# Value products of a softcapped attention in 64x64 quarters, two pairs of heads per turn

## The chip, the core and the metric

The program runs on one core of a Trainium2 chip. The metric is the device time of one execution in microseconds (us). The core's engines run side by side, each through its own list in program order, and wait for one another by semaphores: TensorE (PE, whose weight loads are shown as PEld), ScalarE (ACT), VectorE (DVE), GpSimd (POOL), and SyncE (SP), which here only issues DMAs.

## The reference

```python
# attention: 4 batches, 12 heads, 448 positions, 64 numbers per head
scores = q @ k.T / 8
scores = cap * tanh(scores / cap)
attn = exp(scores - max(scores)); attn = attn / (sum(attn) + 1e-9)
x = (attn @ v), heads side by side            # 1792 x 768
x = relu(x @ moe_w_in) ** 2 @ moe_w_out        # 768 -> 2048 -> 768
out = ((x @ w1) * (x @ w2)) @ w3 @ w_out       # 768 -> 1024 -> 1024 -> 768
```

## The kernel before

The program has two stages. The attention stage takes about the first 240 us; beside attention it multiplies w3 by the last w_out once, so that one product is left at the end ("weight products", L647 to L649: 384 columns, each a sum of three products of numbers split into a high and a low part). Then come the two dense blocks, in which PE works almost without a pause. The change is in the attention stage alone.

Two heads make a pair, two pairs make a quad: there are 24 pairs and 12 quads (d = 0 to 11). Scores are kept transposed, 128 keys on the partitions and 448 queries along each row. The 448 keys of a head are three tiles of 128 and a rest of 64. A *unit* is the two heads' tile of 128 keys (t = 0, 1, 2), or, once per quad, the four rests together (L, t = 3 in the code, `LAST`). So a quad has 7 units and the stage 84; before, their order in a quad is a0 a1 a2 L b0 b1 b2, where a and b are its pairs.

What happens to a unit u:

- `emit_qk`, L479 (L488 for L): four products in 64x64 quarters of PE's array, which run side by side, into a tile `sc` of two PSUM banks. There are two such tiles, so unit u+2 waits for the tanh of unit u.
- `emit_tanh` (L498) on ACT per unit, and `emit_exp` (L504) on ACT for two units at once.
- `emit_sum` (L514, L520) on DVE adds the tiles up over t for the denominators; `emit_den` (L559, and L563 for the first five quads) sums them over the partitions by a product with ones, once per quad.
- `emit_pv` (L533): the value products. For a tile of 128 keys two products of 128 rows by 64 columns of the array, one for each head; for L four of 64x64 (L540). All products of a pair add up in one PSUM bank `pv`, and `evacuate` (L569) copies the bank to `acc` on ACT or DVE.

The loop over u writes every engine's list in this order. At an even u: exp of the two units before, scores of u and u+1, their tanh, then some weight products. At an odd u: the copy of a finished weight product (L660), the value products of units u-5 and u-4, and what `later` holds for this u (copies of finished banks, denominators). I call one even and one odd u a *step*: step e has the scores of units 2e and 2e+1, and the value products of step e stand behind them in PE's list. Between these, pieces of the weights are converted on ACT, DVE and POOL (L119 to L144), and DVE multiplies `acc` by the inverse denominators (L353), which come by way of DRAM in DMAs (`dt`, `rec_d`, `bs`). q and k of a pair are loaded into one of two buffers (`load_qk`), v into one of three (`load_v`).

Of the kernel before, what the change touches and what calls it, by code (L numbers as in the profile page):

```python
# [9 lines left out]
F32 = mybir.dt.float32  # L10
# [4 lines left out]
AF = mybir.ActivationFunctionType  # L15
ALU = mybir.AluOpType
# [5 lines left out]
def tile_kernel(ctx, tc, q, k, v, cap, w_in, w_out, w1, w2, w3t, wo2, out):  # L22
# [31 lines left out]
    GD = 2  # L54
# [375 lines left out]
    with ExitStack() as actx:  # L430
# [13 lines left out]


        sel = stat.tile([128, 32 + GD - 1], F32, name="sel")

        def what(u):

            d, x = divmod(u, 7)  # L450
            return 2 * d + (x > LAST), x if x <= LAST else x - LAST - 1

        def load_qk(p, first=S):

            if p < NPAIR:
                b, hp = divmod(p, NP)
                rk = ap_.tile([128, S], F32, name="rk", bufs=2)
                rq = ap_.tile([128, S], F32, name="rq", bufs=2)
                SP.dma_start(out=rk[:, :first], in_=k[b, hp, :, :first])
                SP.dma_start(out=rq, in_=q[b, hp])  # L460
                if first < S:
                    SP.dma_start(out=rk[:, first:], in_=k[b, hp, :, first:])
                loaded[p] = rk, rq

        def load_v(p):
            if p < NPAIR:
                b, hp = divmod(p, NP)
                vals[p] = ap_.tile([128, NT, D], F32, name="rv", bufs=3)
                SP.dma_start(out=vals[p], in_=v[b, hp])

        def emit_qk(u):

            p, t = what(u)
            sc = ps_s.tile([128, 2, 512], F32, name="sc")
            if t < LAST:
                rk, rq = loaded[p]
                for z, j in product(range(2), range(2)):
                    r, c = slice(j * D, (j + 1) * D), j ^ z
                    PE.matmul(sc[c * D:(c + 1) * D, j, :S], rk[r, 128 * t + c * D:128 * t + (c + 1) * D], rq[r, :], start=True,  # L479
                              stop=True, tile_position=(j * D, c * D))  # L480
                if p % 2 and t == LAST - 1:
                    load_qk(p + 2)
            else:
                for z in range(2):
                    rk, rq = loaded[p + z]
# [4 lines left out]
                load_qk(p + 2)  # L490
# [14 lines left out]

        def emit_sum(u):

            p, t = what(u)
            if t == 0:
                return  # L510
            if t == 1:
                sums[p] = ap_.tile([128, 2, S], F32, name="sum", bufs=3)
            if t < LAST:
                DVE.tensor_tensor(out=sums[p], in0=units[u - 1] if t == 1 else sums[p], in1=units[u], op=ALU.add)  # L514
            z = p % 2
            if p // 2 >= LAST_ADDED and (t == LAST or z and t == 1):
                x = units[u - z * 2]
                for j in range(2):
                    r = slice((j ^ z) * D, (1 + (j ^ z)) * D)
                    DVE.tensor_tensor(out=sums[p][r, j, :], in0=sums[p][r, j, :], in1=x[r, z, :], op=ALU.add)  # L520

        def pv_tile(p):
            pvs[p] = ps_v.tile([128, 512], F32, name="pv")[:, :S]

        def emit_pv(u):

            p, t = what(u)
            x = units[u]
            if t < LAST:
                if t == 0 and p % 2 == 0:  # L530
                    pv_tile(p)
                for j in range(2):
                    PE.matmul(pvs[p][j * D:(j + 1) * D], vals[p][:, 3 * j + t, :], x[:, j, :],  # L533
                              start=t == 0 and p % 2 == 0, stop=t == LAST - 1 and p % 2 == 1, tile_position=(0, j * D))
            else:
                pv_tile(p + 1)
                for z in range(2):
                    for j in range(2):
                        r = slice((j ^ z) * D, (1 + (j ^ z)) * D)
                        PE.matmul(pvs[p + z][j * D:(j + 1) * D], vals[p + z][r, 6, :], x[r, z, :],  # L540
                                  start=z == 1, stop=z == 0, tile_position=((j ^ z) * D, j * D))

        def den_group(p):

# [4 lines left out]
        def emit_den(p):  # L549

            b, g, n = den_group(p)
            c = p % NP // 2 - g
            if c == 0:
                dens[b] = ps_d.tile([128, 512], F32, name="den")[:, :S]
            for z in range(2):
                ps = sums.pop(p + z)
                for j in range(2):
                    r = 32 * (2 * z + j)
                    PE.matmul(dens[b][r:r + 32], sel[:, GD - 1 - c:GD - 1 - c + 32], ps[:, j, :],  # L559
                              start=c == 0, stop=c == n - 1 and p // 2 >= LAST_ADDED, tile_position=(0, r))  # L560
            for z, j in product(range(2), range(2)) if p // 2 < LAST_ADDED else ():
                r, h = 32 * (2 * z + j), slice((j ^ z) * D, (1 + (j ^ z)) * D)
                PE.matmul(dens[b][r:r + 32], sel[h, GD - 1 - c:GD - 1 - c + 32], units[7 * (p // 2) + LAST][h, z, :],  # L563
                          start=False, stop=c == n - 1, tile_position=(h.start, r))

        def evacuate(p):
# [119 lines left out]
        for n in range(3):  # L686
            w_fetch(n)
        load_v(0)
        wprod = w_products()
        wnext, chains, side = 0, [], []  # L690
        products_left = NM * 16
# [2 lines left out]

        later = {}
        for d in range(NPAIR // 2):
            for x, p in ((7 * d + LAST, 2 * d), (7 * d + 6, 2 * d + 1)):
                later.setdefault((x + 4 | 1) + EVAC, []).append(partial(evacuate, p))
            x = (7 * d + 12 | 1) + 2 * (d == NPAIR // 2 - 1)
            later.setdefault(x, []).append(partial(emit_den, 2 * d))  # L700
            later.setdefault(x + EVAC, []).append(partial(store_den, 2 * d))

        for u in range(NU + 10):
            if u < NU and u % 7 in (1, 4):
                load_v(what(u)[0] + 1)
            if 0 <= u - 1 < NU:
                emit_exp(u - 1)
            if u % 2 == 0:
                if u < NU:
                    for x in (u, u + 1):  # L710
                        emit_qk(x)
                    for x in (u, u + 1):
                        emit_tanh(x)
                if w_open:
# [477 lines left out]
```

## Time and profile before

| | |
|---|---|
| median of 3 runs | 1018.32 us (1018.26 to 1018.82) |
| the profiled execution | 1018.64 us, of which the span from its first to its last instruction is 1016.8 |
| PE busy | 1002.5 us, 99% of the span |
| DVE, ACT, POOL busy | 790.1, 549.4, 207.5 us |
| granted PE clock | full (1.00) |

An execution of 1018.64 us is 1.8 us longer than its span. In rows of a timeline a matmul in 32-bit numbers counts as two, so that the four quarter products of a unit appear as x8, and the two 128x64 products as x4; the order of the program counts them once. The end of a matmul is modelled, since matmuls overlap; intervals between starts are what can be relied on. "[1.45 <-PE sc L479]" behind a row says how long its engine had been idle and what ended that.

### The profile page before, as it was taken

The numbers are of one execution on the slowest core, as the hardware profiler recorded it, in microseconds if no ns is written. First come the engines' busy times: TensorE is split into PE (matmuls) and PEld (weight loads), VectorE is DVE, ScalarE is ACT, GpSimd is POOL, SyncE is SP. The second block draws the span as 40 slices with busy tenths as digits, with TensorE's granted clock in tenths as the row PEclk, the third lists the DMA queues.
The fourth block names the chain that finished last, engine by engine and source line by source line (L and its number), as shares of the span: only waits on it lengthen the run. The fifth ranks groups of instructions, "written<-read, shape, count | busy, mean of one in ns | idle before, by whom it ended". The sixth has DMA issues, their size and how long they took to land.

```text
span 1016.8 us, 15085 instructions
## 1 busy us (share of the span) xinstructions
PE 1002.5 (99%) x5410; PEld 827.3 (81%) x5410; DVE 790.1 (78%) x1494; ACT 549.4 (54%) x952; POOL 207.5 (20%) x367
## 2 busy tenths in 40 slices
PE   7999999999999999999999999999999999999998
PEld 1343455566999999999999999999999999999997
DVE  5967988786677989888888887558557788947796
ACT  7999978776786566556655665343241122241100
POOL 3332222221211111111111101002232230333220
PEclk9999999999999999999999999999999999999999
DMA  6567566645456756567576554206577673987662
GB/s 217 180 203 218 179 205 208 198 139 204 125 151 194 223 174 199 188 186 233 171 205 211 175 164 147 63 1 189 166 218 228 208 231 104 332 252 229 215 206 109
DMA packets 82591, 189.35 MB, mean 186 GB/s; under 512 B 10738, under 2 KB 34676, under 8 KB 82516
## 3 DMA queue, kind: packets, MB, share of 16 engines
q0 software_dynamic: 42896, 104.25, 33.1%
q1 hardware_dynamic: 39476, 84.14, 27.1%
q8 instruction: 43, 0.70, 0.3%
q14 instruction: 32, 0.26, 0.1%
q10 hardware_dynamic: 144, 0.00, 0.0%
HBM read 144.53 MB, written 43.82 MB: 185 GB/s over the span
## 4 chain that ended last, share of the span: by engine, by line
PE 86%; DVE 6%; ACT 5%; DMA 1%; issue 1%; POOL 0%; SPq 0%; DVEq 0%; POOLq 0%; ACTq 0%
PE h L361 13%; PE h L360 13%; PE h L362 13%; PE y L361 10%; PE y L360 10%; PE y L362 9%; PE sc L479 3%; PE pv L533 3%; PE h L647 2%; PE h L649 2%; PE h L648 2%; ACT pt L498 1%; ACT pt L504 1%; DVE sum L514 1%; PE y L1007 1%
## 5 line engine op out<-in xcount | busy, mean ns | idle before, releaser
L361 PE MATMUL y<-gl,wb 128*128 128x448 f32 x372 | 135.0, 363 | 0.0
L360 PE MATMUL y<-gh,wb 128*128 128x448 f32 x372 | 134.9, 363 | 0.0
L362 PE MATMUL y<-gh,wb 128*128 128x448 f32 x372 | 134.0, 360 | 0.0
L412 DVE TENSOR_TENSOR acc<-y,acc 128x448 f32<-128x448 f32 x168 | 97.9, 619 | 18.3 <-PE y L362 17.1
L230 POOL DMA_DIRECT2D wc_d<-bs x56 | 30.6, 546 | 268.2 <-DVE bs L86 125.9
L86 DVE TENSOR_TENSOR gl<-gr,gh 128x448 fp32r<-128x448 f32 x78 | 48.4, 620 | 46.7 <-ACT gh L395 42.7
L393 ACT ACTIVATE gr<-h 128x448 f32<-128x448 f32 x62 | 33.4, 539 | 90.0 <-PE h L362 89.6
L360 PEld LDWEIGHTS y<-gh,wb 128*128 128x128 f32 x372 | 69.8, 188 | 5.8 <-ACT acc L410 0.4
L479 PE MATMUL sc<-rq,rk 64*64 64x448 f32 x576 | 66.2, 566 | 8.2 <-DMA rq<-q 4.8
L122 ACT ACTIVATE cvx<-raw 128x384 int32<-128x384 uint32 (+1 forms) x136 | 73.8, 543 | 0.0
L843 POOL DMA_DIRECT2D wb<-wc_d x112 | 59.6, 545 | 68.7 <-PE h L362 43.6
L362 PEld LDWEIGHTS y<-gh,wb 128*128 128x128 f32 x372 | 69.6, 187 | 4.8
L361 PEld LDWEIGHTS y<-gl,wb 128*128 128x128 f32 x372 | 69.8, 188 | 3.7
L361 PE MATMUL h<-x1l,wb 128*128 128x448 f32 x192 | 69.7, 363 | 0.0
L361 PE MATMUL h<-x2l,wb 128*128 128x448 f32 x192 | 69.7, 363 | 0.0
L360 PE MATMUL h<-x1h,wb 128*128 128x448 f32 x192 | 69.5, 362 | 0.0
L360 PE MATMUL h<-x2h,wb 128*128 128x448 f32 x192 | 69.4, 362 | 0.0
L362 PE MATMUL h<-x1h,wb 128*128 128x448 f32 x192 | 69.3, 361 | 0.0
L362 PE MATMUL h<-x2h,wb 128*128 128x448 f32 x192 | 69.3, 361 | 0.0
L119 ACT ACTIVATE cvx<-raw 128x384 f32<-128x384 f32 x124 | 66.8, 539 | 0.0
L360 PE MATMUL h<-x0h,wb 128*128 128x448 f32 x180 | 65.2, 362 | 0.3 <-DVE bt L924 0.3
L142 ACT ACTIVATE wb<-cvx 128x384 fp32r<-128x384 f32 x56 | 29.1, 519 | 67.3 <-DVE cvx L130 39.8
(232 smaller groups left out, 2589.6 us busy)
## 6 DMA issues: line engine op xcount, KB each, us to landing
wb<-wc_d POOLq DMA_DIRECT2D x112, 384.0 KB, 5.7
wc_d<-bs POOLq DMA_DIRECT2D x56, 384.0 KB, 3.2
raw<-wy_d POOLq DMA_DIRECT2D x48, 384.0 KB, 3.6
raw<-w_in SPq DMA_DIRECT2D x32, 384.0 KB, 3.6
raw<-w_out SPq DMA_DIRECT2D x32, 384.0 KB, 3.6
raw<-w SPq DMA_DIRECT2D x32, 384.0 KB, 3.9
wy_d<-spare POOLq DMA_DIRECT2D x25, 384.0 KB, 4.4
raw<-w3t SPq DMA_DIRECT2D x16, 384.0 KB, 4.1
```

The costliest lines, as they stand in the source:

```text
L86: DVE.tensor_tensor(out=l, in0=src, in1=h.bitcast(F32), op=ALU.subtract)
L119: ACT.activation(a, upper, AF.Copy, scale=2.0 ** -112)
L122: ACT.activation(r, words[:, :, 0], AF.Copy, scale=2.0 ** -29)
L230: POOL.dma_start(out=wc_d[m, j], in_=x)
L360: PE.matmul(ps, wh, xh[:, i, :], start=start and i == 0, stop=False)
L361: PE.matmul(ps, wh, xl[:, i, :], start=False, stop=False)
L362: PE.matmul(ps, wl, xh[:, i, :], start=False, stop=(i == n - 1))
L393: ACT.activation(r, h, AF.Relu)
L412: DVE.tensor_tensor(out=a, in0=y, in1=a, op=ALU.add)
L479: PE.matmul(sc[c * D:(c + 1) * D, j, :S], rk[r, 128 * t + c * D:128 * t + (c + 1) * D], rq[r, :], start=True, stop=True, tile_position=(j ...
L533: PE.matmul(pvs[p][j * D:(j + 1) * D], vals[p][:, 3 * j + t, :], x[:, j, :], start=t == 0 and p % 2 == 0, stop=t == LAST - 1 and p % 2 == ...
L843: POOL.dma_start(out=x, in_=wc_d[s % NM, j])
```

## The change

- **Order of the units.** In a quad with even d: a0 a1 b0 b1 L a2 b2; with odd d: a0 b0 a1 b1 L a2 b2. `order` and `unit_of` hold it; sums and denominators look units up there.
- **Value products.** `emit_pv` goes, `emit_turn` comes. In step e the table `GROUPS` (14 steps, repeated three times; an entry is step, quad, half, tiles) says which quad has its turn, which half, and which t. A turn goes over t and for each t issues four 64x64 products (L574, in `pv_product`): both heads of both pairs, each with 64 of the 128 keys. These four use the four quarters of the array. The other 64 keys of the tiles come in another turn, with the other `half`. L is taken whole as before. I call four quarter products one *round*; a quad has 7 rounds, as many as before (where two 128x64 products were one). The last quad is done as before, in 128x64 products, behind all units (L563 of the new file).
- **A wait.** If the quad has already had a turn, the first product of the turn waits for the tanh of unit 2e ("fence" below).
- **PSUM banks** of both pairs are taken together, and both are copied out right behind the quad's last turn; before, each pair's copy came one step after its last product.
- **Loads.** Three tiles from the pool `cv` are a third buffer for q and k (every third pair) and a fourth for v (every fourth). `load_qk(p + 3)` is issued with the last scores of pair p; v of a quad is loaded when the quad two before it is done.

```diff
+        third = [cv.tile([128, S], F32, name="bt", bufs=3) for _ in range(3)]
+        ORDERS = "a0 a1 b0 b1 L a2 b2", "a0 b0 a1 b1 L a2 b2"
...
+        GROUPS = [(3, 0, 0, "01"), (4, 0, 1, "01"), (5, 0, 0, "2L"), (6, 0, 1, "2"), (7, 1, 0, "01L"), (8, 1, 1, "012"), (9, 1, 0, "2"),
...
-                if p % 2 and t == LAST - 1:
-                    load_qk(p + 2)
+                if t == LAST - 1:
+                    load_qk(p + 3)
...
-            ACT.activation(pt, units[u], AF.Tanh, scale=scl)
+            tanhs[u] = ACT.activation(pt, units[u], AF.Tanh, scale=scl)
...
+        def emit_turn(e):
...
+            d, half, what = turns[e]
+            if "0" in what and 2 * d not in pvs:
+                pv_tile(2 * d)
+                pv_tile(2 * d + 1)
...
+            fence = tanhs[2 * e]
+            for t, z, j in product(what, range(2), range(2)):
+                t = LAST if t == "L" else int(t)
+                i = pv_product(2 * d + z, j, j ^ z ^ (0 if t == LAST else half), t, d not in begun and t == 0, done_at[d] == e and t == (LAST if what[-1] == "L" else int(what[-1])))
+                if fence and d in begun:
+                    tc.add_manual_dep(i.ins, fence.ins.name, mybir.DependencyInfo(mybir.DependencyClass.Sync, mybir.DependencyReason.DATA),
+                                      reason="the other row half of the array has finished with this bank")
+                fence = None
+            begun.add(d)
...
+        def pv_product(p, j, h, t, start, stop):
...
+            r = slice(h * D, (h + 1) * D)
...
+            v, x = (vals[p][r, 6, :], units[unit_of[d, LAST]][r, p % 2, :]) if t == LAST else (vals[p][r, 3 * j + t, :], units[unit_of[p, t]][r, j, :])
+            return PE.matmul(pvs[p][j * D:(j + 1) * D], v, x, start=start, stop=stop, tile_position=(r.start, j * D))
...
-            for x, p in ((7 * d + LAST, 2 * d), (7 * d + 6, 2 * d + 1)):
-                later.setdefault((x + 4 | 1) + EVAC, []).append(partial(evacuate, p))
+            for z in range(2):
+                later.setdefault(2 * done_at[d] + 1, []).append(partial(evacuate, 2 * d + z))
+                later.setdefault(2 * done_at[d] + 3, []).append(partial(load_v, 2 * d + 4 + z))
...
-                for x in (u - 5, u - 4):
-                    if 0 <= x < NU:
-                        emit_pv(x)
+                emit_turn(u // 2)
```

Three places show what moves. The first is PE's list from the value products of step 15 to the denominators of step 16. Before (`pv` rows are value products, `sc` rows scores, `h` rows weight products, `den` denominators):

```order
L533 MATMUL pv<-pt,rv 64x448 x4
L479 MATMUL sc<-rq,rk 64x448 x8
L647 MATMUL h<-wb,w3h 128x384
L648 MATMUL h<-wb,w3h 128x384
L649 MATMUL h<-wb,w3l 128x384
L533 MATMUL pv<-pt,rv 64x448 x4
L559 MATMUL den<-sum,sel 32x448 x4
L563 MATMUL den<-pt,sel 32x448 x4
```

And after, from the last of the four rounds of step 15 on (`bt` are the new buffers):

```order
L574 MATMUL pv<-pt,rv 64x448 x2
L574 MATMUL pv<-pt,bt 64x448 x2
L503 MATMUL sc<-bt 64x448 x2
L503 MATMUL sc<-rq,rk 64x448 x2
L494 MATMUL sc<-bt 64x448 x4
L680 MATMUL h<-wb,w3h 128x384
L681 MATMUL h<-wb,w3h 128x384
L682 MATMUL h<-wb,w3l 128x384
L574 MATMUL pv<-pt,rv 64x448 x2
L574 MATMUL pv<-pt,bt 64x448 x2
L592 MATMUL den<-sum,sel 32x448 x4
L596 MATMUL den<-pt,sel 32x448 x4
```

Step 15 had two rounds and has four, step 16 had two and has one, and between value products and scores the shape of the products no longer changes.

The second place is PE's list around step 30, which has no weight products. Before, from the value products of step 29 to the scores of step 31:

```order
L533 MATMUL pv<-pt,rv 64x448 x4
L479 MATMUL sc<-rq,rk 64x448 x8
L533 MATMUL pv<-spare,rv 64x448 x4
L559 MATMUL den<-sum,sel 32x448 x4
L479 MATMUL sc<-rq,rk 64x448 x8
```

And after, from the third of step 29's four rounds:

```order
L574 MATMUL pv<-pt,rv 64x448 x2
L574 MATMUL pv<-pt,bt 64x448 x2
L574 MATMUL pv<-pt,rv 64x448 x2
L574 MATMUL pv<-pt,bt 64x448 x2
L503 MATMUL sc<-rq,rk 64x448 x2
L503 MATMUL sc<-bt 64x448 x2
L494 MATMUL sc<-rq,rk 64x448 x4
L574 MATMUL pv<-pt,rv 64x448 x2
L574 MATMUL pv<-pt,bt 64x448 x2
L592 MATMUL den<-sum,sel 32x448 x4
L494 MATMUL sc<-bt 64x448 x4
L494 MATMUL sc<-rq,rk 64x448 x4
```

The value products of step 30, which now wait for the tanh of unit 60, stand directly behind the scores of units 60 and 61.

The third place is ACT's list at the end of the stage, where the operands of the first dense block are split (`x0h`, `x1h`; `gh` is its first result). Before:

```order
L569 ACTIVATE acc_72<-pv 128x448
L504 ACTIVATE spare<-spare,capt 128x1792
L322 ACTIVATE x0h<-acc_69 128x448 x3
L569 ACTIVATE acc_72<-pv 128x448
L322 ACTIVATE x0h<-acc_69 128x448 x3
L322 ACTIVATE x1h<-acc_70 128x448 x2
L393 ACTIVATE cvx<-sc 128x448
L394 ACTIVATE cvx<-cvx 128x448
L395 ACTIVATE gh_2510<-cvx 128x448
L569 ACTIVATE acc_72<-pv 128x448
L322 ACTIVATE x1h<-acc_70 128x448 x4
```

And after:

```order
L602 ACTIVATE acc_72<-pv 128x448
L518 ACTIVATE spare<-spare,capt 128x1792
L322 ACTIVATE x0h<-acc_69 128x448 x3
L602 ACTIVATE acc_72<-pv 128x448 x2
L322 ACTIVATE x0h<-acc_69 128x448 x3
L322 ACTIVATE x1h<-acc_70 128x448 x2
L393 ACTIVATE cvx<-sc 128x448
L394 ACTIVATE cvx<-cvx 128x448
L395 ACTIVATE gh_2622<-cvx 128x448
L322 ACTIVATE x1h<-acc_70 128x448 x4
```

The last pair's copy has moved from behind `gh` to before the second three of `x0h`.

## Rows read from the trace of the kernel before

**Rows 1.** Stretches: start:end length, busy us of PE, PEld, DVE, ACT, POOL; clock.

```profile
10.00:50.00 40.00, 36.77 (x267) 10.94 (x263) 35.77 (x65) 38.17 (x42) 14.96 (x11) 1.00 0.61 194
50.00:100.00 50.00, 49.45 (x348) 18.74 (x340) 36.98 (x72) 49.07 (x63) 12.85 (x24) 1.00 0.69 203
...
150.00:200.00 50.00, 50.00 (x338) 28.65 (x336) 38.42 (x75) 39.82 (x55) 12.72 (x24) 1.00 0.61 190
```

**Rows 2.** What PE waited for up to 250 us: total, times, longest.

```profile
PE sc L479 <- DMA rq<-q: 4.8, 1, 4.8
```

**Rows 3.** Groups by form: quarter value products, busy us, mean ns.

```profile
L540 PE MATMUL pv<-pt,rv 64*64 64x448 f32 x64 | 7.9, 562 | 0.0
```

**Rows 4.** Timeline of PE, step 31 to 32: start, length, instructions.

```profile
166.29 0.97 PE L533 MATMUL pv<-spare,rv 128*64 128x448 f32 x4
167.19 0.98 PE L540 MATMUL pv<-spare,rv 64*64 64x448 f32 x8
167.99 1.68 PE L479 MATMUL sc<-rq,rk 64*64 64x448 f32 x16
169.60 0.44 PE L647 MATMUL h<-wb,w3h 128*128 128x384 f32 x1
```

**Rows 5.** Timeline of PE, steps 13 to 16.

```profile
63.06 1.72 PE L533 MATMUL pv<-spare,rv 128*64 128x448 f32 x8
...
66.49 1.73 PE L479 MATMUL sc<-rq,rk 64*64 64x448 f32 x16
...
76.24 1.72 PE L533 MATMUL pv<-pt,rv 128*64 128x448 f32 x8
77.89 1.74 PE L479 MATMUL sc<-rq,rk 64*64 64x448 f32 x16
```

**Rows 6.** Timeline of ACT: tanh of steps 10, 13, 16 and 17.

```profile
49.97 1.91 ACT L498 ACTIVATE spare<-sc,scl 128x896 f32<-128x896 f32 x2 [1.45 <-PE sc L479]
...
63.84 1.91 ACT L498 ACTIVATE pt<-sc,scl 128x896 f32<-128x896 f32 x2
...
78.94 1.91 ACT L498 ACTIVATE spare<-sc,scl 128x896 f32<-128x896 f32 x2
...
84.75 1.91 ACT L498 ACTIVATE spare<-sc,scl 128x896 f32<-128x896 f32 x2 [0.92 <-PE sc L479]
```

**Rows 7.** Chain of waits, 80 to 125 us: start, length, what.

```profile
81.03 0.53 DVE acc L569
...
87.90 4.74 DMA rec_d<-dt
...
93.72 6.40 DMA bs<-rec_d
...
118.34 0.44 DVE cvt L130
118.80 0.42 ACT w3h L142
...
124.53 0.39 ACT cvt L660
```

**Rows 8.** Timeline around step 30, PE and ACT.

```profile
157.00 1.72 PE L533 MATMUL pv<-pt,rv 128*64 128x448 f32 x8
...
160.10 1.89 ACT L498 ACTIVATE pt<-sc,scl 128x896 f32<-128x896 f32 x2
```

**Rows 9.** Timeline of PE behind the attention stage.

```profile
243.21 0.47 PE L361 MATMUL sc<-x0l,wb 128*128 128x448 f32 x1 [0.59 <-DVE x0l L86]
...
251.25 0.48 PE L361 MATMUL sc<-gl,wb 128*128 128x448 f32 x1 [0.66 <-DVE gl L86]
```

**Rows 10.** Timeline of DVE: copies behind quads 0 and 1, a pause.

```profile
32.54 0.61 DVE L569 COPY acc<-pv 128x448 f32<-128x448 f32 x1
...
45.36 0.62 DVE L569 COPY acc<-pv 128x448 f32<-128x448 f32 x1
...
66.09 0.42 DVE L86 TENSOR_TENSOR w3l<-cvt,w3h 128x256 fp32r<-128x256 f32 x1 [3.54 <-ACT w3h L142]
```

More of the change, by code (lines that the diff above doesn't have):

```diff
@@ L446, in tile_kernel @@
         sel = stat.tile([128, 32 + GD - 1], F32, name="sel")
-        def what(u):
-            d, x = divmod(u, 7)
-            return 2 * d + (x > LAST), x if x <= LAST else x - LAST - 1
+        tanhs, begun = {}, set()
+        third = [cv.tile([128, S], F32, name="bt", bufs=3) for _ in range(3)]
+        ORDERS = "a0 a1 b0 b1 L a2 b2", "a0 b0 a1 b1 L a2 b2"
+        order = []
+        for d in range(NPAIR // 2):
+            for x in ORDERS[d % 2].split():
+                order.append((2 * d, LAST) if x == "L" else (2 * d + (x[0] == "b"), int(x[1])))
+        unit_of = {x: u for u, x in enumerate(order)}
+        GROUPS = [(3, 0, 0, "01"), (4, 0, 1, "01"), (5, 0, 0, "2L"), (6, 0, 1, "2"), (7, 1, 0, "01L"), (8, 1, 1, "012"), (9, 1, 0, "2"),
+                  (10, 2, 1, "01"), (11, 2, 0, "01L"), (12, 2, 1, "2"), (13, 2, 0, "2"), (14, 3, 1, "01"), (15, 3, 0, "01L2"), (16, 3, 1, "2")]
+        turns, done_at = {}, {}
+        for c, (e, d, half, what) in product(range(NPAIR // 8), GROUPS):
+            e, d = e + 14 * c, d + 4 * c
+            if 2 * e < NU:
+                turns[e] = d, half, what
+            done_at[d] = e
+        turns[NU // 2], turns[NU // 2 + 1] = (NPAIR // 2 - 1, None, "01"), (NPAIR // 2 - 1, None, "L2")
+        done_at[NPAIR // 2 - 1] = NU // 2 + 1
         def load_qk(p, first=S):
@@ L456, in load_qk @@
                 b, hp = divmod(p, NP)
-                rk = ap_.tile([128, S], F32, name="rk", bufs=2)
-                rq = ap_.tile([128, S], F32, name="rq", bufs=2)
+                rk, rq = third[:2] if p % 3 == 2 else (ap_.tile([128, S], F32, name=x, bufs=2) for x in ("rk", "rq"))
                 SP.dma_start(out=rk[:, :first], in_=k[b, hp, :, :first])
@@ L467, in load_v @@
                 b, hp = divmod(p, NP)
-                vals[p] = ap_.tile([128, NT, D], F32, name="rv", bufs=3)
+                vals[p] = third[2].rearrange("p (t d) -> p t d", t=NT) if p % 4 == 3 else ap_.tile([128, NT, D], F32, name="rv", bufs=3)
                 SP.dma_start(out=vals[p], in_=v[b, hp])
         def emit_qk(u):
-            p, t = what(u)
+            p, t = order[u]
             sc = ps_s.tile([128, 2, 512], F32, name="sc")
@@ L506, in emit_sum @@
         def emit_sum(u):
-            p, t = what(u)
+            p, t = order[u]
             if t == 0:
@@ L513, in emit_sum @@
             if t < LAST:
[L514 to L518, printed above, removed]
+                DVE.tensor_tensor(out=sums[p], in0=units[unit_of[p, 0]] if t == 1 else sums[p], in1=units[u], op=ALU.add)
+            if p // 2 < LAST_ADDED:
+                return
+            w = unit_of[p - p % 2, LAST]
@@ L519, in emit_sum @@
+            for z in range(2) if t == LAST else (p % 2,) if t == 1 and w < u else ():
+                for j in range(2) if p - p % 2 + z in sums else ():
                     r = slice((j ^ z) * D, (1 + (j ^ z)) * D)
-                    DVE.tensor_tensor(out=sums[p][r, j, :], in0=sums[p][r, j, :], in1=x[r, z, :], op=ALU.add)
+                    x = sums[p - p % 2 + z][r, j, :]
+                    DVE.tensor_tensor(out=x, in0=x, in1=units[w][r, z, :], op=ALU.add)
         def pv_tile(p):
             pvs[p] = ps_v.tile([128, 512], F32, name="pv")[:, :S]
[L525 to L541, printed above, removed]
@@ new lines, in emit_turn @@
+        def emit_turn(e):
+            if e not in turns:
+                return
+            d, half, what = turns[e]
+            if "0" in what and 2 * d not in pvs:
+                pv_tile(2 * d)
+                pv_tile(2 * d + 1)
+            if half is None:
+                for t in what:
+                    if t == "L":
+                        for z, j in product(range(2), range(2)):
+                            pv_product(2 * d + z, j, j ^ z, 3, False, False)
+                        continue
+                    for p, j in product((2 * d, 2 * d + 1), range(2)):
+                        PE.matmul(pvs[p][j * D:(j + 1) * D], vals[p][:, 3 * j + int(t), :], units[unit_of[p, int(t)]][:, j, :],
+                                  start=t == "0", stop=t == "2", tile_position=(0, j * D))
+                return
+            fence = tanhs[2 * e]
[7 more added lines that the diff above has]
+            begun.add(d)
@@ L703, in tile_kernel @@
         for u in range(NU + 10):
-            if u < NU and u % 7 in (1, 4):
-                load_v(what(u)[0] + 1)
+            if u in (1, 5, 7):
+                load_v({1: 1, 5: 2, 7: 3}[u])
             if 0 <= u - 1 < NU:
@@ L709, in tile_kernel @@
                 if u < NU:
-                    for x in (u, u + 1):
-                        emit_qk(x)
+                    emit_qk(u)
+                if u < NU:
+                    emit_qk(u + 1)
                     for x in (u, u + 1):
```

5 lines of the change are left out of this document (3 added, 2 removed).

## The prediction

> **What bounds the kernel now.** I read the view of stretches first. After 50 us PE is busy for 49.45 and 50.00 of 50 us, in the dense blocks too, so what the change is worth is the time by which the attention stage, about 240 us, ends earlier or later. The first 100 us are a close race of three: ACT is busy for 49.07 of the 50 us up to 100, and DVE for 35.77 of the 40 up to 50 [rows 1]. Then PE alone is full. Next the list of what PE waited for: in 250 us one DMA, at the very start [rows 2]. A third buffer for q and k has no wait to remove, and I cost it at nothing: by the code they are issued three units or more ahead of their use, after as before. Third the timelines, PE beside ACT. In the first 105 us ACT has hardly a gap but two where it waits for scores, 1.45 and 0.92 us, both after a step with denominators [rows 6]; there PE is the late one. Last the chain of waits from 80 to 125 us: it runs through a copy of value products on DVE at 81.03, two DMAs of the inverse denominators, a stretch of DVE and then ACT, which ends with the copy of a weight product at 124.53 [rows 7]. PE's next weight products start at 124.96, since they need that bank. So up to 125 us a saving on PE alone is not one of time; from 125 us to the end PE is the bound.
>
> **Work of the array: unchanged.** A round is four 64x64 products after and two 128x64 products before, seven to a quad in both. From 166.29 to 167.19 a round and a change of shape take 0.90 us; from 167.19 to 169.60 a round of 64x64 value products, two rounds of 64x64 scores and a change take 2.41 [rows 4]. So a round is (2.41 - 0.90) / 2 = 0.755 us and a change of shape 0.145; two rounds of 128x64 and a change, 76.24 to 77.89, are 1.65 [rows 5], a change of 0.14. I take 0.15. Twice as many weight loads cost nothing, since PEld has 28.65 busy us in 50 [rows 1].
>
> **Changes of shape.** Value products and scores now have the same shape. Counted in PE's list, up to the first product of the dense block, 136 changes become 96. Of the 40 that go, 25 stand ahead of the weight products of step 25 (124.96 us), where the chain holds the end, and 15 behind: 15 x 0.15 = -2.25 us. If quarter products of different kinds drained like different shapes, it would be 0 (rival C).
>
> **Rounds that come later.** Value products start one step later (step 3 for step 2) and the table shares them out unevenly. Up to step 24 the old list has 23 steps x 2 = 46 rounds, the new one 44 (28 in the first fourteen steps, then 2, 2, 2, 1, 3, 3, 1, 2). Two rounds move from where PE is not the bound to where it is: 2 x 0.755 = +1.5 us.
>
> **The fence.** The first product of a turn now waits for the tanh of unit 2e, except in a quad's first turn. What is queued behind it on PE is the rest of the turn, denominators and the next scores, for which ACT waits. From step 25 on the steps with weight products have 6 to 24 of them ahead of it, and the tanh is over in time. Two fenced steps have none (30 and 36). In step 30: turn 29 starts at 157.00 [rows 8] and now has four rounds, so the scores of unit 60 start at 157.00 + 4 x 0.755 = 160.0 and PE is through with both units at 161.5. A tanh starts 1.05 after its scores (77.89 to 78.94 [rows 5, 6]) and lasts 1.0 (two take 1.91): it ends at 162.05, a wait of 0.55. ACT, which reached it at 160.10 before [rows 8], doesn't make it later. Step 36 has three rounds ahead and comes to about the same: together +1.1. Bounds: 0, if the tanh comes sooner behind its scores, and 2 x 1.0, a whole tanh each.
>
> **The stage in which ACT and DVE share the bound.** Here I follow steps 13 to 16. In step 13 the value products started at 63.06, before that step's tanh at 63.84 [rows 5, 6]. Now they wait for its first half, until 64.85, and one round and the denominators (66.49 - 63.06 - 1.65 = 1.8) bring the next scores to 67.4 instead of 66.49. From there to 76.24 PE had no pause; two changes fewer leave turn 15 at 76.85. It has four rounds where two were: the scores of step 16 start at 79.85 instead of 77.89, their tanh at 80.9 instead of 78.94, and turn 16, fenced on it, starts at 81.9 and ends at 82.7. Behind it DVE's copy of the bank, which ran at 81.03 in the midst of DVE's own work, now waits till then: +1.7 us at a link of the chain to 124.53, and a link has no slack in it [rows 7]. So the weight products of step 25 start 1.7 later. In return step 16 has one round before its denominators instead of two, and ACT's later waits go.
> The bounds: the best is that both waits of ACT go, since every step with denominators now has one round, and the fence costs nothing: -(1.45 + 0.92) = -2.4. The worst adds DVE's copies behind quads 0 and 1: they ran at 32.54 and 45.36 [rows 10], in a stretch where DVE has few gaps, and would wait for fenced turns too, for as long as the third at most: 2 x 1.7, so +5.1. I take +1.7: DVE stood idle for 3.54 us before 66.09 [rows 10], where the first two can be made up, but not the third.
>
> **The end of the stage.** Eight rounds with denominators follow the last weight products where six did; the two more are counted above. PE's waits there, 0.59 and 0.66 us [rows 9], are for operands that ACT and DVE split; PE arrives later against them, so the first goes. The last pair's copy no longer stands on ACT behind `gh`, ahead of the work that the second wait hangs on: of that I take 0.4, somewhat less than the 0.62 of such a copy on DVE [rows 10]. The copy now holds up the second three of `x0h`, which I cost at nothing, as PE works through the first three meanwhile; without that cover it is the two copies' time, 1.2. Together -1.0; bounds -1.25 and +1.2.
>
> **Sum.** +1.7 - 2.25 + 1.5 + 1.1 - 1.0 = +1.05. Made against the profiled execution (1018.64 us: a span of 1016.8 and 1.8 around it) that is 1019.7; this execution is 0.3 above the median of the runs, 1018.32, so on their footing 1019.4 us.
>
> **Rivals.**
> *A, the fence is free and the early stage gains.* ACT's two waits go and nothing takes their place: -2.4 - 2.25 + 1.5 + 1.1 - 1.0 = -3.05, so 1015.3; with the two waits of 1.1 gone as well, 1014.2. For it: every step with denominators has only one round, just where ACT waited. Against: step 15 with 15 weight products and four rounds, and the chain over the DMAs, which PE doesn't shorten.
> *B, slower: DVE, waiting in order for the banks.* Copies stand right behind the last turn, whose start hangs on ACT. If DVE can't make up the first two, their 3.4 us come on top: 1022.8; half made up, 1021.1. It decides from where DVE is later by more than the pause before 66.09. Against: PE never waited for DVE before 240 us [rows 2], and the weights it makes are several steps ahead.
> *C, the change doesn't save what it says:* quarter products of one kind drain behind those of another as two shapes do. Then -2.25 is 0: 1021.6. Against it stands the 0.80 of a 64x64 round before scores (167.19 to 167.99), beside 0.90 with a change [rows 4].
> *D, two row halves at one bank take turns.* Each round's products for one pair come from both row halves into one bank. If these exclude each other, 84 rounds less the last quad's 7 double: 77 x 0.755 = +58 us, 1077. Against: L's products did the same before, at 562 ns of mean length [rows 3] in rounds of 0.80 to 0.90 [rows 4]. The Trainium skill, "TensorEngine Tiling (Array Packing)", section "Restrictions and Gotchas", says that different row tiles cannot access the same PSUM bank simultaneously and that software must synchronise. By that rule D would hold; the rows of L speak against it where the two halves write different partitions, and for the same partitions the fence keeps the turns apart.
>
> **Chances.** My forecast 0.50, A 0.21, B 0.19, C 0.07, D 0.03. A measurement of this kernel tells about 0.2% from no change, that is 1016.3 to 1020.4. Of A 0.18 are faster than that and 0.03 within; of my forecast 0.02 faster, 0.43 within and 0.05 slower; of B 0.03 within and 0.16 slower; C and D are slower. Together faster 0.20, same 0.49, slower 0.31. The range goes from A's 1015.3 to 1022.3; C and most of B lie in it, D and the outer ends of A and B are left out.
>
> **What would show it.** In the profile after: a step from the last value products to the scores' start without 0.15 us over the rounds; the scores of step 16 about 2 us later than 77.89; DVE idle before a copy of `pv`, released by PE, of 1 us or more; PE idle, released by a tanh, in steps 30 and 36, about half a us each; the first product of the dense block about 2 us later than before, and no wait for `x0l` behind it. The prediction is wrong if turn 15 doesn't push the scores behind it, if the chain to 125 us goes past the copy at 81 us, or if PE's list from step 25 on is not shorter by changes and longer by two rounds.

## The result and the profile after

The changed kernel takes 1025.99 us (median of 4 runs, 1022.86 to 1026.93) and the kernel before, on the same chip, 1018.29 us: a ratio of 1.0069, with a 95% interval from 1.0050 to 1.0088. The forecast was 1019.4 and no change; the kernel is 7.7 us slower. The profiled execution took 1026.46 us, a span of 1024.7 against 1016.8.

Where these 7.9 us of span come in, by the PE timeline: the value products of step 25 start at 130.15 instead of 128.32 (+1.8); the last value products end at 244.8 instead of 240.9 (+3.9); the first dense product starts at 247.43 instead of 240.81 (+6.6); the rest is behind that.

First the list of what PE waited for in the first 300 us (total us, times, longest), which answers to [rows 2]:

```profile
PE pv L574 <- ACT pt L512: 5.1, 8, 1.7
PE sc L494 <- DMA rq<-q: 4.8, 1, 4.8
PE sc L360 <- DMA wb<-w_d: 2.6, 1, 2.6
...
PE pv L574 <- ACT spare L512: 2.2, 3, 1.4
...
PE h L361 <- DVE x3l L86: 0.7, 1, 0.7
PE sc L361 <- DVE gl L86: 0.2, 1, 0.2
```

Two rows are new and large: value products that wait for a tanh (the fence, 7.3 us in 11 pauses), and the first dense products, which wait for a DMA. The wait for x0l of [rows 9] is gone and that for gl is down from 0.66 to 0.2, but x3l has taken a place.

The timelines of steps 13 to 16 answer to [rows 5] and [rows 6]. PE:

```profile
64.91 0.59 PE L574 MATMUL pv<-pt,rv 64*64 64x448 f32 x2 [1.17 <-ACT pt L512]
...
67.59 1.74 PE L494 MATMUL sc<-bt 64*64 64x448 f32 x16
...
76.99 0.59 PE L574 MATMUL pv<-spare,rv 64*64 64x448 f32 x2
77.00 0.59 PE L574 MATMUL pv<-spare,bt 64*64 64x448 f32 x2
...
80.04 0.54 PE L503 MATMUL sc<-bt 64*64 64x448 f32 x2
```

and ACT:

```profile
81.04 1.90 ACT L512 ACTIVATE spare<-sc,scl 128x896 f32<-128x896 f32 x2 [1.78 <-PE sc L503]
```

Turn 13, which ran at 63.06 before, now starts at 64.91, and the scores behind it at 67.59. The four rounds of turn 15 (76.99 to 80.04, 3.05 us with no change of shape) push the scores of step 16 to 80.04, and ACT stands idle for 1.78 us until they come. These three starts are within 0.2 us of the forecast.

But steps 13 to 16 are not where most of the fence is. Ahead of step 25 eight turns pause for a tanh, 6.2 us together, and the longest pause is in step 19:

```profile
97.43 1.74 PE L574 MATMUL pv<-spare,rv 64*64 64x448 f32 x16 [1.73 <-ACT pt L512]
```

The chain of waits, which answers to [rows 7], has changed its engines. These are pieces of it from 60 to 105 us:

```profile
63.95 0.91 ACT pt L512
64.91 0.98 PE pv L574 x8
...
77.06 3.17 PE pv L574 x32
80.22 0.80 PE sc L503 x7
81.04 1.90 ACT spare L512 x2
...
100.84 0.91 ACT pt L512
101.80 0.98 PE pv L574 x8
```

From 60.35 us to the weight products of step 25 it runs through ACT and PE alone, and the turns that wait for a tanh (13 and 20 here) are links of it. DVE's copy behind turn 16 does come late, at 83.45 after a wait of 1.96 us for PE, but it is no link any more.

What the forecast did not see is at the end of the stage. DVE and SyncE (SP) in the changed kernel:

```profile
238.24 0.62 DVE L602 COPY acc<-pv 128x448 f32<-128x448 f32 x1 [10.13 <-PE pv L574]
238.78 0.55 DVE L86 TENSOR_TENSOR w3l<-cvt,w3h 128x384 fp32r<-128x384 f32 x1
```

```profile
239.35 0.32 SPq L665 DMA_DIRECT2D w_d<-w3l  x1
239.72 1.38 SPq L99 DMA_DIRECT2D raw<-w_in  x3
241.15 5.10 SPq L775 DMA_DIRECT2D wb<-w_d  x8
```

The same two steps on DVE and SP in the kernel before:

```profile
232.33 0.56 DVE L86 TENSOR_TENSOR w3l<-cvt,w3h 128x384 fp32r<-128x384 f32 x1 [7.28 <-ACT w3h L142]
```

```profile
234.73 4.88 SPq L739 DMA_DIRECT2D wb<-w_d  x8
```

DVE stands for 10.13 us at the copy of quad 10's first pair, whose last turn ends at 238. Behind it, in DVE's order, is the subtraction that makes the last w3l piece; ACT had its w3h ready at 234.9. That piece is stored by SP, and SP's next entries are three loads of `raw` and then the 8 loads of the first dense block's weights. So these go out from 241.15 instead of 234.73, and PE pauses. Then the clock (stretches of the changed kernel: length, busy us of PE, PEld, DVE, ACT, POOL; granted clock, DMA share, GB/s) and the products in it:

```profile
247.43 0.44 PE L360 MATMUL sc<-x0h,wb 128*128 128x448 f32 x1 [2.62 <-DMA wb<-w_d]
...
249.27 0.58 PE L362 MATMUL sc<-x0h,wb 128*128 128x448 f32 x1
249.64 0.58 PE L360 MATMUL sc<-x0h,wb 128*128 128x448 f32 x1
```

```profile
16.00:20.00 4.00, 3.72 (x24) 1.44 (x28) 3.83 (x8) 4.00 (x5) 3.11 (x2) 0.60 0.84 276
248.00:252.00 4.00, 4.00 (x15) 3.62 (x14) 3.01 (x6) 0.00 (x0) 0.57 (x1) 0.62 1.04 408
```

From 248.91 to 252.25 nine products start 0.37 us apart (3.34 us) instead of 0.20 (1.8): 1.5 us at the lower of the clock's two levels, 1.2 GHz, behind a pause of 2.62 us. The clock falls in the same way at 16 us, behind a pause of 2.48, when PE has no value products yet; there ACT is busy for 4.00 of the 4 us, and nothing is lost: with all of DVE's copies later (below) the clock stayed at 1.00 in this stretch, and the scores of step 5 start at 25.70 there and at 25.67 here.

### The profile page after: what moved, and what is told of

It reads as the page before. It is cut to its first block, busy times and chain, and to the rows that moved or that the text cites. A ratio compares the mean times of both kernels' runs of the same rounds, so it can differ in the third digit from the quotient of the medians.

```text
span 1024.7 us, 15599 instructions
## 1 busy us (share of the span) xinstructions
PE 1000.8 (98%) x5674; PEld 834.3 (81%) x5674; DVE 789.2 (77%) x1494; ACT 550.6 (54%) x952; POOL 207.9 (20%) x367
## 4 chain that ended last, share of the span: by engine, by line
PE 86%; ACT 5%; DVE 5%; DMA 2%; issue 1%; SPq 0%; POOL 0%; DVEq 0%; POOLq 0%; ACTq 0%
PE h L361 13%; PE h L360 13%; PE h L362 13%; PE y L361 9%; PE y L360 9%; PE y L362 9%; PE pv L574 4%; PE sc L494 3%; PE h L680 2%; PE h L681 2%; PE h L682 2%; ACT pt L512 1%; ACT pt L518 1%; PE y L1041 1%; PE den L592 1%
## 5 line engine op out<-in xcount | busy, mean ns | idle before, releaser
L361 PE MATMUL h<-x0l,wb 128*128 128x448 f32 x180 | 65.3, 363 | 0.0
```

The source lines that it names most:

```text
L361: PE.matmul(ps, wh, xl[:, i, :], start=False, stop=False)
```

## The experiments

The theory after the result: two costs, the fence (in 28 of the 42 steps the first value product has to wait for a tanh) and the late copy in DVE's order. Rivals: the loads are late by themselves; DVE's in-order copies also set the stage up to 125 us (rival B); the fence costs only its visible pauses behind step 25. Each kernel was timed against the kernel before on the same chip. The edits are shortened: plain words and `...` in them stand for code that is left out.

**One copy later** (quad 10's first pair, DVE):

```
-  2 * done_at[d] + 1
+  2 * done_at[d] + (2 if 2 * d + z == NPAIR - 4 else 1)
```

> One copy of value products on VectorE (the first pair of quad 10) is issued two instructions later, behind the w3l subtraction and one sum. Nothing else moves. Theory (VectorE, waiting in order for that bank, holds up the w3l subtraction, with it the store of the last w0 piece, the 8 loads behind it on SyncE's queue, and TensorE's first dense products): w3l runs at about 234.9 us instead of 238.8, the wait of 2.6 us for the loads goes, TensorE has no pause there and its granted clock stays 1.00 from 247 to 255 us (about 1.5 us more). The wait of 0.7 us for x3l stays or grows a little. Time 1025.99 - 2.6 - 1.5 = 1021.9 us, range 1021 to 1023. Rival (the loads are late by themselves, behind other transfers): the wait shrinks by less than 1 us, 1025 to 1026 us.

Measured 1023.12 us, ratio 1.0047 [1.0035, 1.0060]: 2.9 us less than the changed kernel; 4.1 were expected, and the time is just above the expected range. DVE, then the stretch behind the first dense product (at 244.19, with no wait):

```profile
234.35 0.56 DVE L86 TENSOR_TENSOR w3l<-cvt,w3h 128x384 fp32r<-128x384 f32 x1 [6.79 <-ACT w3h L142]
234.83 1.08 DVE L528 TENSOR_TENSOR sum<-pt 128x896 f32<-128x896 f32 x1
237.68 0.62 DVE L602 COPY acc<-pv 128x448 f32<-128x448 f32 x1 [1.77 <-PE pv L574]
```

```profile
244.00:248.00 4.00, 3.42 (x15) 2.44 (x14) 4.00 (x8) 3.00 (x7) 0.00 (x0) 1.00 1.04 407
```

The pause and the fall of the clock are gone with the one instruction's place; the wait of 0.6 for x0l came back. The first dense product starts 3.2 us earlier, and the rival (loads late by themselves) falls. The 2.9 itself is uncertain, since the four runs of the changed kernel spread over 4.1 us; the same edit is tried a second time below.

**All of DVE's copies later** (`ON_ACT` stands for the copies that ACT makes):

```
-  2 * done_at[d] + 1
+  2 * done_at[d] + (1 if ON_ACT else 2)
```

> All of VectorE's copies of value products (quads 0 to 10) are issued one half step later, behind the conversions and the sum that stood behind them. Theory (VectorE's waiting for banks also set the stage up to 125 us, there worth the 1.8 us by which the weight products of step 25 start later): as with the last copy alone, and about 1.8 us less: 1020.1 us, range 1019 to 1021.5; VectorE's idle time released by value products falls from 35.8 us to under 10. Rival 1 (that stage is later through the four rounds and the fence on TensorE, not through VectorE's copies): the same time as with the last copy alone, 1021.9. Rival 2 (the banks come free later and TensorE, which needs them in the next step, waits for the copies): TensorE's waits for copies of 0.5 us and more in several steps, 1023 or more.

Measured 1024.04, ratio 1.0054 [1.0041, 1.0066]: a miss, 3.9 us above the expected time. Up to step 19 the scores start where they did with one copy later (93.36 and 93.39 us), and from step 20 on they start later (step 25 at 126.49 and 125.33). So freeing DVE from its waits for banks gained nothing in the early stage. With the chain above, in which no copy of DVE stands, rival B of the prediction falls there. Further on the later copies hold banks that PE needs, as the second rival said:

```profile
170.93 1.88 PE L574 MATMUL pv<-spare,rv 64*64 64x448 f32 x14 [1.76 <-DVE acc L602]
```

**128x64 turns without a fence**, in the same table and order:

```
+  PE.matmul(pvs[p]..., vals[p][:, 3 * j + int(t), :], units[unit_of[p, int(t)]][:, j, :], ..., tile_position=(0, j * D))
-  fence = tanhs[2 * e]
```

> Same units, same turns and same copies, but a turn takes 128x64 products of one pair (pair a where it took half 0, pair b where it took half 1), with no fence on a tanh; L's products stay 64x64. The array changes its shape 38 times more often, about 15 of them behind step 25. Theory (fence 1.15 us of pauses behind step 25 and up to 1 us before it, a change of shape 0.15 us, the late last copy 4 us): 1025.99 - 1.15 - 0.5 + 15 x 0.15 = 1026.6 us, range 1025 to 1028, and the first dense product still waits for its loads. Rival (the fence is what made the kernel slower): 1021 or less. Second rival (a change of shape costs nothing): 1024.3.

Measured 1021.46, ratio 1.0027 [1.0017, 1.0037]: 5 us under what I expected, close to the rival. The scores of step 26, which start at 132.46 in the changed kernel, start at 129.23 (before: 129.98), those of step 41 at 227.59 (231.19; before 228.92). The order of units and the table are ahead of the kernel before. The late copy is still there: the first dense product waits 2.43 us for its loads.

```profile
129.23 0.93 PE L494 MATMUL sc<-rq,rk 64*64 64x448 f32 x8
...
243.66 0.47 PE L360 MATMUL sc<-x0h,wb 128*128 128x448 f32 x1 [2.43 <-DMA wb<-w_d]
```

**Both undone**: 128x64 turns, and the one copy later.

> The 128x64 turns without a fence, and the one copy issued later, together. Theory (two separate costs: the fence through all of the stage, the late copy at its end): the wait for loads of 2.4 us before the first dense product goes, the granted clock stays 1.00 behind it (about 1.5 us), the wait of 0.6 us for x0l comes back: 1021.46 - 2.4 - 1.5 + 0.6 = 1018.1 us, range 1017.3 to 1019.3, within 0.2% of the kernel before. Rival (both are one cost, and the first hides the second): 1021 or more.

Measured 1019.10, ratio 1.0003 [0.9994, 1.0012], within the expected range: 2.4 us less than with the early copy, and here the two intervals don't touch. It is the same time as the kernel before. From 25 to 240 us PE has no pause at all.

**128x64 turns with the fence:**

```
+  fence = tanhs[2 * e] if d in opened else None
+  tc.add_manual_dep(first product of the turn, fence)
```

> The 128x64 turns, now with the same fence as the changed kernel: the first product of a turn waits for the tanh of the step's first unit, except in a quad's first turn. The copies stand as in the changed kernel. Against the kernel without the fence (1021.46) the difference is what the fence costs; against the changed kernel (1025.99) it is what the quarters save in changes of shape. Theory (a change of shape 0.15 us, 15 of them behind step 25): 1028.2 us, fence 6.8 us. Rival 1 (the quarters save nothing that counts, the fence costs 4.5 us): 1026.0. Rival 2 (the fence costs nothing, the quarters themselves are slower): 1021.5.

Measured 1027.00, ratio 1.0084 [1.0071, 1.0098], between the theory and rival 1. Against 1021.46 the fence costs 5.5 us (7.0 at the first dense product, 250.62 against 243.66; the kernel without it gives 1.5 back behind a fall of the clock, which this one doesn't have). Against the changed kernel the quarters save 3.2 us at that same product; there the clock gives 1.5 back and a wait for x3l 0.7, and the 1.0 that is left in the medians is less than the spread of the runs. Of the 7.0 us, 6.5 are lost by the scores of step 26:

```profile
135.69 0.93 PE L494 MATMUL sc<-rq,rk 64*64 64x448 f32 x8
...
250.62 0.45 PE L360 MATMUL sc<-x0h,wb 128*128 128x448 f32 x1 [2.22 <-DMA wb<-w_d]
```

**The kernel before with the fence and nothing else** (28 of 42 steps):

```
+  if u % 2 == 0 and 2 * e < NU and e > 2 and (e - 3) % 14 not in (0, 4, 7, 11):
+      tc.add_manual_dep(first value product of the step, tanhs[2 * e])
```

> The kernel before with nothing but such a fence: in 28 of its 42 steps (all but those at which the changed table starts a quad) the first value product waits for the tanh of the step's first unit. Theory (the fence costs by itself, since TensorE has no other work in a step with few weight products, and ScalarE then gets its next scores later): 4 to 6 us, 1022.4 to 1024.4. Rival (it costs only together with the uneven table, above all in turns of four rounds): under 1.5 us, 1019.9 or less.

Measured 1025.63, ratio 1.0068 [1.0055, 1.0080]: 7.0 us slower than the kernel before on that chip (1018.59), 1.2 us above the expected range. The fence alone makes the kernel before as slow as the changed one. Its PE in steps 12 and 13, then its ACT in steps 12, 14 and 15:

```profile
62.19 1.72 PE L536 MATMUL pv<-spare,rv 128*64 128x448 f32 x8 [1.35 <-ACT pt L498]
63.85 1.74 PE L479 MATMUL sc<-rq,rk 64*64 64x448 f32 x16
66.58 1.72 PE L536 MATMUL pv<-spare,rv 128*64 128x448 f32 x8 [0.27 <-ACT pt L498]
```

```profile
61.12 1.92 ACT L498 ACTIVATE pt<-sc,scl 128x896 f32<-128x896 f32 x2
...
71.06 1.90 ACT L498 ACTIVATE pt<-sc,scl 128x896 f32<-128x896 f32 x2 [0.36 <-PE sc L479]
...
76.31 1.91 ACT L498 ACTIVATE pt<-sc,scl 128x896 f32<-128x896 f32 x2 [0.79 <-PE sc L479]
```

Without the fence the value products of step 12 ran at 58.66, ahead of that step's tanh at 59.49, in the time in which ACT converts weights and takes exponentials. With it that work of PE (1.65 us, more with denominators) moves behind half the tanh, into the time in which PE should make the next scores; they come late, and ACT then waits for them (0.36, 0.79). The pauses of value products on PE add up to 8.6 us in the list of waits, a little more than the 7.0 that they cost.

**Denominators ahead of the turn**, to cover the fence:

```
+  for f in todo: if f.func is emit_den: f()
   emit_turn(u // 2)
```

> In the steps that have denominators, these stand ahead of the value products and not behind them. They last 0.9 us, so the fence's wait of 0.38 us (steps 30, 37) is covered, and value products stand right before the scores: one change of shape less in ten steps, about five of them behind step 25. Theory: -0.8 - 5 x 0.15 = -1.5 us, and a little of the stage before 125 us: 1024.3 us, range 1023.3 to 1025.5; the late last copy stays (it is behind the last turn, which then is 0.9 us later against it, but so is the work behind it). Rival (denominators wait for VectorE's sums, which stood 1.06 us too late in step 37, and hold up the turn and the scores): TensorE's pauses before denominators grow to 1 us and more in several steps, 1027 or more.

Measured 1030.07, ratio 1.0116 [1.0103, 1.0130]: a miss, 4 us slower than the changed kernel. Value products that wait for a tanh cost 9.4 us instead of 7.3, and one row of denominators waits 1.6 for DVE's sum. The rival was right in kind, since the work put ahead waits itself, but in one step and not in several. Why the waits of value products grew was not followed.

**The turn between the scores of the next step's two units:**

```
   emit_qk(u)
+  emit_turn(u // 2 - 1)      # fence: tanhs[2 * e + 1]
   emit_qk(u + 1)
```

> The changed kernel's quarters and table, but a turn stands one half step later, between the scores of the next step's two units, and its fence is the tanh of the second unit of the step before, which then is nearly over (the scores in front of the turn wait for that step's first tanh anyway); VectorE's and ScalarE's copies follow. The last three turns and quad 10's copies stand as in the run with the last copy later. Theory (the fence costs its 5 to 7 us only by where the turn stands, with nothing on TensorE between the scores and the tanh): no wait for a tanh of over 0.4 us before value products; beside the 128x64 turns with the late copy (1019.1 us) the array changes shape 47 times less, about 18 of them behind step 25: 1019.1 - 18 x 0.15 = 1016.4 us, range 1014.5 to 1018.5, faster than the kernel before. Rival (any turn that waits for ScalarE and stands ahead of scores makes ScalarE wait for these in turn): 1021 us or more, and ScalarE's waits for scores over 6 us in the first 125 us.

Measured 1024.35, ratio 1.0059 [1.0047, 1.0072]. No value product waits for a tanh any more, and yet it is 1.2 us above the run with one copy later: the expected 1016.4 was wrong by 8. The waits moved to the scores (10.9 us for ACT in all, 3.8 in the changed kernel), and in the four-round turn ACT waits again:

```profile
81.70 1.01 ACT L512 ACTIVATE spare<-sc,scl 128x896 f32<-128x896 f32 x1 [1.46 <-PE sc L494]
```

ACT's waits for scores from 20 to 126 us are 4.4, not the 6 of the rival; how the rest divides was not followed further.

**A table one step earlier**, 128x64 turns without a fence, two rounds in most steps:

```
+  TABLE = {2: "a0 a1", 3: "b0 b1", 4: "a2 L", 5: "b2", 6: "a0 a1", 7: "b0 b1 L", 8: "a2 b2", ...}
```

> 128x64 turns without a fence, in a table of their own: first turn in step 2, two rounds a step but for 1 and 3 in four of fourteen, one round fewer behind the last weight products than now, quad 10 done in step 40 and so its copies ahead of the conversions that the last loads hang on. Theory: as the kernel with the 128x64 turns and the late copy, less one round of 0.75 us and about half a us in the early stage where steps of four rounds held the scores up: 1017.1 us, range 1016.0 to 1018.4. Rival (the end of the stage is set by operands that ScalarE and VectorE make, and TensorE only waits longer): 1018 to 1019 us, with waits for x0l and gl of over 0.8 us.

Measured 1025.26, ratio 1.0066 [1.0053, 1.0080]: 8 above the forecast, 6.2 above the 128x64 turns with the later copy. PE's waits for ACT grow from 3.8 to 8.8 us. This table has two rounds where the changed one has a single round beside denominators, so the uneven table may be worth something. That is argued and not shown, since the copies moved too, and which step loses how much was not separated.

**The kernel before with the third buffer for q and k alone** (loads issued a pair earlier):

```
-  load_qk(p + 2)
+  load_qk(p + 3)      # rk, rq = third[:2] if p % 3 == 2
```

> The kernel before with the third buffer for q and k alone, whose loads are issued a pair earlier. Theory (nothing waits for these loads after the first): the same time, 1018.3 to 1018.9 us. Rival (the earlier loads stand in the way of others on SyncE's queue in the first 20 us, or the first units' conversions get their words earlier): a difference of over 1 us either way.

Measured 1018.50, ratio 0.9996 [0.9987, 1.0006]: nothing, as costed.

**Quarters only behind weight products**, in quads 6, 8 and 10, 128x64 turns elsewhere, one copy later:

```
+  if half is not None and d not in (6, 8, 10):      # 128x64, no fence
```

> 128x64 turns without a fence for quads 0 to 5, 7 and 9, the quarters with their fence for quads 6, 8 and 10, whose fenced turns stand behind 6 to 24 weight products; quad 10's copy later. Theory (behind weight products the tanh is over and the fence costs nothing, so only the saved changes of shape remain, 10 of them, in a stretch where TensorE alone is the bound): 1019.1 - 10 x 0.15 = 1017.6 us, range 1016.8 to 1018.4, just faster than the kernel before. Rival (a fence costs also behind weight products): 1019.5 or more.

Measured 1018.22, ratio 0.9998 [0.9989, 1.0007]: within the expected range, 0.9 us less than with 128x64 turns throughout (1019.10), where 1.5 were expected. No value product pauses for a tanh in it.

**The same with quads 6 to 10** (`d not in (6, 7, 8, 9, 10)`):

> As before it, with the quarters and their fence for quads 7 and 9 too. That brings back the three fenced turns without enough weight products ahead (steps 30, 36, 37; waits of 0.38 us each and 1.06 us at denominators behind the last in the changed kernel) and saves 8 more changes of shape. Theory: 1017.6 + 1.15 + 1.06 - 8 x 0.15 = 1018.6 us, range 1017.6 to 1019.6. Rival (behind step 25 the fence costs as much as ahead of it, two thirds of a us in each fenced turn): 1020 or more.

Measured 1017.80, ratio 0.9994 [0.9985, 1.0003], within the expected range. This kernel differs from the run with one copy later only in quads 0 to 5: 1023.12 - 1017.80 = 5.3 us, so that is what the fence costs there, net of the saved changes of shape. Behind step 25 its three short pauses stand in the list of waits and on the timeline:

```profile
PE pv L585 <- ACT pt L512: 1.1, 3, 0.4
```

```profile
203.50 0.59 PE L585 MATMUL pv<-spare,rv 64*64 64x448 f32 x2 [0.35 <-ACT pt L512]
204.41 1.04 PE L603 MATMUL den<-sum,sel 128*32 128x448 f32 x8
```

The third, 0.35 us in step 37, stands behind nine weight products. The rival falls: 1017.80 and 1018.22 are not measurably apart, so what the pauses cost and what the eight changes of shape bring come to about the same. Neither version is measurably faster than the kernel before.

## Why the prediction was wrong

Taken away one after the other, the parts of the change are worth 2.9 us for the late copy, 5.3 for the fence in quads 0 to 5, and -0.7, which is within the noise, for all the rest (1017.80 against 1018.49). These are three pieces of one difference, so they add up in any case. What bears them out is that with 128x64 turns the late copy is worth 2.4 us and the whole fence 5.5.

Beside the terms of the sum, by the profiled executions: the stage up to step 25 was forecast at +1.7 and came to +1.8; the stretch from there to the last value product at +0.35 and came to +2.1; the end of the stage and the dense block behind it at -1.0 and came to about +4.0. Step by step:

- **Changes of shape, -2.25.** Right in count: by the trace 56 changes become 41 from step 25 to the dense block. Somewhat less in size: in the last kernel that stretch takes 113.56 us (126.45 to 240.01) against 112.49 before; with two rounds (1.51) and three pauses (1.1) more, 15 changes have brought 1.5, about 0.1 each. This is worked out from that one stretch and not measured change by change. Rival C is out.
- **Two rounds later, +1.5**, as the trace shows: eight rounds behind the last weight products, six before.
- **The fence in steps 30 and 36, 0.55 each.** Pauses of 0.38 there and 0.39 in step 37, 1.15 in all where I had 1.1; that the totals agree is luck. I had said that behind weight products the tanh is over in time, and step 37 pauses behind nine of them. It has a second delay that I did not price: its denominators last 2.02 us in the changed kernel (0.96 before, 1.04 in the last one), since DVE's sum came late, behind a wait of 0.88 for a DMA. That is the larger part of what the stretch behind step 25 costs over the forecast.
- **The stage shared by ACT and DVE, +1.7.** The size came out (+1.83 at step 25), and that is luck, for the mechanism did not. I let the fence act in step 13 and on turn 16 and took DVE's copy for the link that passes it on. The chain of the changed kernel goes past that copy, which I had named as a sign of being wrong, and eight turns pause ahead of step 25, not one. The runs show two large terms of opposite sign. Without the fence the order and its table reach step 25's value products at 126.77 (128x64 turns) instead of 128.32: 1.55 of the 2.4 us of rival A's gain. The fence takes 6.5 us by step 26 in 128x64 turns, and the quarters get 3.2 of them back. Issuing DVE's copies later gained nothing there. My reading of [rows 2] was short as well: besides the DMA the list has seven waits for ACT, 3.9 us together, five of them in the first 30 us, so ACT already held PE up there.
- **The end of the stage, -1.0: the step that failed.** I followed the waits for x0l and gl and the copies of the last pair, and came to -1.0 where the runs have about +4.0; x0l's wait did go and gl's shrank. But I had priced DVE's waiting, in rival B, at the copies behind quads 0, 1 and 3 only. The one that counted was quad 10's, ten us of waiting with the first dense block's weights behind it on DVE and SP: 2.6 us of pause and 1.5 of lower clock. (PE's wait for x3l, 0.7, is not all its doing: 0.37 of it is left with the copy later, and why was not followed.) I had named what is queued behind the waiting instruction on PE, and not what is queued behind this copy on DVE. My "PE never waited for DVE before 240 us [rows 2], and the weights it makes are several steps ahead" was true of the weight products and false of the last stored piece.
- **Rival D** is out. The Trainium skill, "TensorEngine Tiling (Array Packing)", section "Restrictions and Gotchas", says that different row tiles can't use one PSUM bank at the same time. Where the two halves write different partitions of the bank, the trace disagrees: in turn 15 the rows at 76.99 and 77.00 hold the products of both heads of either pair, which come from the two row halves into one bank, and the four rounds take 3.05 us, 0.76 each, as forecast for rounds that run side by side. For the same partitions no run here shows it, since the fence stands in every kernel whose quarters write there from both halves.

The range ended at 1022.3, just short of rival B's worst of 1022.8, and all of B's delays were in the early stage; a cost at the stage's end had no case of its own but the copies' 1.2 us.

## What to carry to other kernels

A semaphore wait that keeps two uses of one engine apart is priced at every place of the loop in which it stands, and not in one worked step: by what that engine did in the time that it now waits, and by who waits for it next. This one cost 7 us in a kernel in which it was the only edit. Before a copy is put right behind its producer on an in-order engine, look at the entry behind it for every copy of the loop, the last one first, and follow it through the DMA queue to the next stage. Where a wait must be, put it behind work that is long enough. In the changed kernel fenced turns behind 6 to 24 weight products did not pause, but for the one in step 37, which paused for 0.39 us behind nine.

## What the runs showed of the hardware

The granted clock fell to 0.50 (1.2 GHz) behind a pause of 2.62 us of PE in the changed kernel, and behind one of 2.43 with the 128x64 turns, for about 3.4 us each; with the fenced 128x64 turns a pause of 2.22 left it at 1.00. Pauses of 2.5 us at 14 to 16 us were followed by a fall in some kernels (the changed one, 0.60 from 16 to 20 us) and by none in others (1.00 with the 128x64 turns, first row below). With both costs undone the clock was at 0.50 from 13 to 15 us (second row), behind a pause of only 1.73:

```profile
16.00:20.00 4.00, 3.54 (x24) 0.90 (x24) 3.83 (x7) 4.00 (x5) 2.63 (x2) 1.00 0.81 268
13.00:15.00 2.00, 2.00 (x12) 0.33 (x8) 1.65 (x4) 2.00 (x3) 0.38 (x1) 0.50 0.30 72
```

So the length of the pause does not decide by itself; what does was not tested. The changed kernel's four runs spread over 4.1 us where those of the kernel before spread over 0.7, and the fastest of the four, 1022.86, had the highest mean clock (0.998 against 0.995 and 0.996). It is as fast as the runs with one copy later, so what the late copy costs may differ from one execution to the next.
